# Earlier partial sums of the last 512 output rows, the turned exp sums first in TensorE's queue, and new scheduler settings, in a fused spectral-filter and attention kernel

## The chip, the cores and the metric

The kernel runs on one core of a Trainium2 chip. Its time is the device time of one launch in microseconds (us), and the figures quoted are medians of several launches. On one core most launches agree within 0.3%.

The engines are TensorE (PE in the profile; PEld is its weight loads), VectorE (DVE), ScalarE (ACT), GpSimd (POOL) and SyncE (SP). PSUM is the memory that matmuls write to; the program uses it as eight banks of 512 float32 columns. SBUF is the on-chip memory that holds everything else.

## The reference

Two independent problems on 2048 x 640 bf16 inputs are put side by side in one output of 2048 x 1280:

```python
def _A_ref(x, w_r, w_i):                       # spectral filter, columns 0:640
    X = rfft2(x.astype(float32)) * (w_r + 1j * w_i)
    return irfft2(X, s=(2048, 640)).astype(bfloat16)

def _B_ref(x, wqkv, wo):                       # attention, columns 640:1280
    H, Dh = 32, 20
    q, k, v = ...                              # from x @ wqkv
    p = softmax(q @ k.T * Dh ** -0.5)          # 32 heads of 2048 x 2048
    return (p @ v).transpose(...).reshape(2048, 640) @ wo
```

The softmax has 32 x 2048 x 2048 elements, and every one of them needs an exp. That sets the length of the kernel.

## The kernel before

The program is not written in its order of execution. A scheduler runs when the kernel is built: it keeps a simulated clock for each engine, asks at each step what that engine could do next, and fixes the order in each engine's queue. `occupy(engine, duration)` advances the simulated clock, so the durations in the code are assumptions. On the chip an engine works through its queue in this order and waits on semaphores: in the kernel before, a matmul whose input was ready at about 844.9 us ran only at 848.56, behind 28 others that stood ahead of it in TensorE's queue.

The attention is cut into 32 units: four blocks of 512 queries by eight groups (`g`) of four heads. Scores are made in tiles of 128 keys x 512 queries, 2048 of them. Most go through ScalarE's exp in groups of three and two tiles (PSUM banks 0 to 2, and 3 to 4). Some go in pairs through VectorE:

```python
def try_exp(self):
    i = self.nexp
    if i >= self.nqk or self.qk_t[i] > self.now or self.pt_free[i % NPT] > self.now:   # NPT = 6 buffers
        return False
    ...
    h = 3 * (i % 2)
    pt = self.PT[i % NPT][:, 0:512 * n]
    in_ = self.ps[:, h:h + n, :].rearrange("p b n -> p (b n)")
    self.P.add("act", lambda e: e.activation(pt, in_, AF.Exp, scale=SCALE, bias=-15.0 / LOG2E), ...)
```

The product with V goes to bank 6. At the end of a unit VectorE copies that bank out (`unit_copy`). For the units before the last one, the exp sums then take a way over DRAM, and the output product of each finished block of 512 queries runs as background work. The last unit (`u == 31`) has nothing to hide behind, so its end is a special path, the tail:

```python
def tail_jobs(self):                            # background, before the last exp
    for qb in range(2, 4):                      # row blocks 2 and 3 of the last 512 rows
        for half in range(2):                   # 320 output columns each
            for g in range(NG - 1):             # seven of the eight groups, summed in PSUM
                ... e.matmul(o, OTn[:, g, rows of qb], wo_pad[:, g, half], start=(g == 0), stop=(g == NG - 2))
            # one copy to SBUF:  self.part[:, qb - 2, half]
    # blocks 0 and 1 are summed in the tail itself, 2 x 2 x 7 = 28 matmuls:
    self.tail_op = [(0, half, g) for half in range(2) for g in range(NG - 1)] + [(1, half, g) ...]

def tail_pe(self):                              # TensorE's choice in the tail
    if self.tail_op:                            # 1. the 28 matmuls
        ...
        if ok:
            self.tail_mm(qb, half, g)
            return True
    ...                                         # 2. turned sums: osb (sums in one row of 32) by a
    #    selection matrix -> 128 x 16 in bank 2, so that VectorE takes 16 columns of reciprocals
    #                                             3. spread of 1/sum to all partitions ("tail_spread")
    #                                             4. last group's output matmuls, once VectorE has
    #                                                multiplied ("tail_norm", one per row block)

def tail_add(self, qb, half):                   # blocks 2 and 3: PSUM + kept part -> output rows
    self.P.add("dve", lambda e: e.tensor_tensor(o, a, b, ALU.add), ...)
    self.occupy("dve", 470.0)
```

"Turned" means that TensorE brings the exp sums, which lie along rows, onto all 128 partitions (the rows of the on-chip memories), so that VectorE can take the reciprocals of 16 columns and not of whole rows. "Spread" means that TensorE then brings each reciprocal to all the partitions that have to be multiplied by it.

At the very end VectorE computes a flag: whether any exp sum left the range in which this fast program is exact. All engines load the flag and branch on it, and a second, slower program follows for the case that it is set. With this input it never is.

```python
fast = FK(nc, arena, *args, cfg=dict(LEAD=28, T_A=760000.0, WARM_SHARE=0.45, RUN=1, PVQ=12, WIN=1000.0,
          T_X=40000.0, AHEAD=45e3, T_RB=9000.0, SKIP=1, ALONE=1200.0, PVB=10, PTB=6, WARMUP=10))
```

These settings steer the scheduler. `WARM_SHARE` and `WIN` say when filler matmuls with no use but to keep TensorE's clock up are put in, and hold some background work back too. `LEAD`, `SKIP`, `ALONE` and `T_X` govern which score tiles go to VectorE, and `T_A` how fast the spectral problem is worked off.

## Time and profile before

The median of the first three runs was 860.89 us (860.78 to 861.23). The profiled launch divides as follows. "Exps" means the exp instructions on ScalarE, L1783 of the kernel; they carry the whole kernel.

| part of the profiled launch | us |
|---|---|
| span | 859.8 |
| until the first exp starts | 10.56 |
| first exp start to last exp end | 831.15 |
| of that, gaps between exps (ScalarE idle) | 8.39 |
| last exp's end to the end of the program (tail) | 18.05 |

A group line of the profile has busy time and the mean duration in ns after the bar, then the idle time of that engine before these instructions and whom it waited for. A timeline line has start, duration, engine, source line, operation, shapes and count; in brackets stands the idle time before it and who ended it. When a line merges several instructions, its duration runs from the first start to the last end.

### The profile page before, as it was taken

Reading aid. Unit: us, or ns where it says so; the run is one execution under the profiler, and the core shown is the slowest. Engines: PE = TensorE matmul, PEld = TensorE weight load, DVE = VectorE, ACT = ScalarE, POOL = GpSimd, SP = SyncE. Lnnn points to the kernel's source line nnn. Section 1 sums busy time; section 2 is a strip of 40 time slices with the busy share of each in tenths; the row PEclk is TensorE's granted clock in tenths of the full one; section 3 lists DMA queues with packets and bytes.
Section 4 is the critical chain, followed back from the end, with each engine's and each line's share of the span. In section 5 each row is a group of like instructions: output and inputs, shape, how many; then the busy total and the mean of one; then the engine's idle time right before and its main releaser. Section 6 shows DMA issues by size and latency. Waiting matters only on the chain.

```text
span 859.8 us, 18764 instructions
## 1 busy us (share of the span) xinstructions
PE 809.8 (94%) x8000; PEld 281.2 (33%) x8000; DVE 765.2 (89%) x1485; ACT 830.1 (97%) x738; POOL 2.9 (0%) x8
## 2 busy tenths in 40 slices
PE   8999999999899999999999998989999999999995
PEld 4334323334233333322233422222333332333323
DVE  3487799999897999999998899999999889999972
ACT  6999999999999999999999999999999999999992
POOL 1000000000000000000000000000000000000000
PEclk9999999999999999999999999999999999999998
DMA  7420000001401000010101000001011101011210
GB/s 243 120 61 14 2 14 14 14 14 27 152 14 45 14 14 14 6 47 14 50 14 37 23 6 9 14 14 49 5 38 50 37 22 33 6 37 45 75 44 34
DMA packets 34462, 32.00 MB, mean 37 GB/s; under 512 B 13892, under 2 KB 28484, under 8 KB 34372
## 3 DMA queue, kind: packets, MB, share of 16 engines
q1 hardware_dynamic: 33796, 30.21, 11.3%
q8 instruction: 64, 1.05, 0.5%
q10 hardware_dynamic: 576, 0.52, 0.2%
q14 instruction: 26, 0.21, 0.1%
HBM read 24.97 MB, written 5.50 MB: 35 GB/s over the span
## 4 chain that ended last, share of the span: by engine, by line
ACT 58%; DVE 26%; PE 15%; issue 1%; DVEq 0%; POOL 0%; POOLq 0%
ACT arena L1783 57%; DVE arena L227 6%; DVE arena L1857 4%; PE ps L1766 4%; DVE arena L1253 3%; PE ps L2032 2%; PE ps L1952 2%; DVE arena L1897 2%; DVE arena L1901 2%; DVE arena L1904 2%; PE ps L1581 1%; DVE arena L1895 1%; DVE arena L1899 1%; DVE arena L1893 1%; PE ps L1662 1%
## 5 line engine op out<-in xcount | busy, mean ns | idle before, releaser
L1783 ACT ACTIVATE arena<-ps 128x1536 bf16<-128x1536 f32 x725 | 822.8, 1355 | 7.4 <-PE ps L1766 6.8
L1766 PE MATMUL ps<-arena 32*128 32x512 bf16 x2048 | 309.8, 385 | 26.8 <-ACT arena L1783 14.4
L1952 PE MATMUL ps<-arena 128*32 128x512 bf16 (+3 forms) x2048 | 190.5, 386 | 0.8 <-DVE arena L227 0.4
L1857 DVE TENSOR_SCALAR arena<-ps 128x512 uint16<-128x512 f32 x236 | 162.1, 688 | 13.3 <-PE ps L1766 12.2
L1766 PEld LDWEIGHTS ps<-arena 32*128 32x128 bf16 x2048 | 77.5, 91 | 264.9 <-ACT arena L1783 185.3
L227 DVE CAST arena<-ps 128x320 bf16<-128x320 f32 (+3 forms) x190 | 104.2, 548 | 19.8 <-PE ps L1610 9.9
L1646 PE MATMUL ps<-arena 128*32 128x512 bf16 x964 | 89.6, 389 | 1.6 <-DVE arena L1972 1.4
L1897 DVE TENSOR_TENSOR arena<-arena 128x1024 f16<-128x1024 uint16 x118 | 81.3, 690 | 1.0
L1901 DVE TENSOR_TENSOR arena<-arena 128x1024 f16<-128x1024 f16 x118 | 81.1, 688 | 0.9
L1904 DVE TENSOR_TENSOR arena<-arena 128x1024 uint16<-128x1024 uint16 x118 | 80.9, 687 | 0.2
L1952 PEld LDWEIGHTS ps<-arena 128*32 128x32 bf16 (+1 forms) x2048 | 46.1, 93 | 74.3 <-issue 61.3
L1525 DVE TENSOR_SCALAR arena<-ps,arena 128x512 bf16<-128x512 f32 x61 | 49.3, 808 | 19.9 <-PE ps L1581 14.1
L227 DVE COPY arena<-ps 128x1024 bf16<-128x1024 bf16 (+4 forms) x59 | 42.4, 721 | 19.3 <-PE ps L540 7.7
L1581 PE MATMUL ps<-arena 128*32 128x512 bf16 x640 | 51.0, 383 | 0.7 <-DVE arena L227 0.6
L1895 DVE TENSOR_SCALAR arena<-arena 128x1024 f16<-128x1024 uint16 x118 | 49.8, 424 | 0.7
L1899 DVE TENSOR_SCALAR arena<-arena 128x1024 f16<-128x1024 uint16 x118 | 49.7, 422 | 0.6
L1893 DVE TENSOR_SCALAR arena<-arena 128x1024 uint16<-128x1024 uint16 x118 | 49.8, 424 | 0.5
L1662 PE MATMUL ps<-arena 128*32 128x512 bf16 x640 | 49.3, 382 | 0.4 <-DVE arena L227 0.3
L1646 PEld LDWEIGHTS ps<-arena 128*32 128x32 bf16 x964 | 23.2, 94 | 47.2 <-issue 38.9
L1334 PE MATMUL ps<-arena 128*128 128x320 bf16 (+1 forms) x192 | 38.3, 303 | 0.1
L2032 PE MATMUL ps<-arena 128*128 128x320 bf16 x192 | 36.7, 302 | 0.2 <-DVE arena L1857 0.2
L1610 PE MATMUL ps<-arena 128*128 128x80 bf16 (+1 forms) x320 | 32.2, 236 | 0.0
(74 smaller groups left out, 438.6 us busy)
## 6 DMA issues: line engine op xcount, KB each, us to landing
arena<-rscr SPq DMA_DIRECT2D x31, 256.0 KB
arena<-in_A_x_dram SPq DMA_DIRECT2D x4, 640.0 KB, 6.9
out_dram<-arena SPq DMA_DIRECT2D x4, 640.0 KB, 3.4
out_dram<-arena SPq DMA_DIRECT2D x15, 160.0 KB, 1.8
arena<-f_ciCS SPq DMA_DIRECT2D x8, 256.0 KB, 2.9
arena<-arena SPq DMA_DIRECT2D x124, 2.0 KB, 1.7
arena<-in_B_x_dram SPq DMA_DIRECT2D x3, 640.0 KB, 5.5
arena<-f_cslab SPq DMA_DIRECT2D x2, 768.0 KB, 4.4
```

The lines of the kernel that those rows point to most:

```text
L227: return eng.tensor_copy(out, in_)
L1581: inst = e.matmul(ps[32 * j:32 * j + 32, bank, :], self.wqkv[:, cbv, c:c + 32], r_, start=st, stop=sp, tile_position=(0, 32 * j))
L1646: i = e.matmul(ps[32 * j:32 * j + 32, 6, :], z, k, start=False, stop=False, skip_group_check=True, tile_position=(0, 32 * j))
L1766: inst = e.matmul(ps[:, bank, :], kt_[32 * j:32 * j + 32, g, kt * 128:(kt + 1) * 128], q[32 * j:32 * j + 32, :], start=True, stop=True, ti ...
L1783: self.P.add("act", lambda e: e.activation(pt, in_, AF.Exp, scale=SCALE, bias=-15.0 / LOG2E), r=[("ps", h + k) for k in range(n)], w=[("PT ...
L1857: self.P.add("dve", lambda e: e.tensor_scalar(v, in_, 1024.0 * SCALE * LOG2E, 31743.0, ALU.mult, ALU.min), r=[("ps", bank)], **({"w": [key ...
L1893: t = self.x_op(n, one, lambda e: e.tensor_single_scalar(sh, v, 6, ALU.logical_shift_left), [kv], [ka], "x_s")
L1895: t = self.x_op(n, one, lambda e: e.tensor_scalar(b16, sh, -2.0 ** -24, 2.0 ** -8, ALU.mult, ALU.add), [ka], [kb], "x_l")
L1897: t = self.x_op(n, two, lambda e: e.tensor_tensor(b16, sh, b16, ALU.mult), [ka, kb], [kb], "x_q")
L1901: t = self.x_op(n, two, lambda e: e.tensor_tensor(b16, b16, a16, ALU.mult), [ka, kb], [kb], "x_h")
L1904: t = self.x_op(n, two, lambda e: e.tensor_tensor(v, v, b16, ALU.add), [kb, kv], [kv], "x_w")
L1952: inst = e.matmul(ps[32 * j:32 * j + m, 6, :], va[:, kt, 21 * h:21 * h + m], pt, start=st, stop=sp, tile_position=(0, 32 * j))
```

## The change

The intent is to shorten the tail. There are four parts.

1. Six groups (instead of seven) of **all four** row blocks are summed as background work and kept in SBUF. In blocks 0 and 1 the kept part goes back into PSUM by a float32 matmul with the identity; in blocks 2 and 3 VectorE adds it.
2. In `tail_pe` the turned sums and the spread now come ahead of the remaining output matmuls.
3. Three assumed durations of the scheduler's clock are altered.
4. Seven settings are altered.

The background sums are also asked for one unit earlier (`u == 29`), at another priority (-4.0e4 instead of -1.0e5; not in the cut below).

```diff
-                return (mkev, 0.0, 1.0417 * ne + 124, kw, ...)          # spectral multiply, assumed ns
+                return (mkev, 0.0, 1.0417 * ne + 155, kw, ...)
...
-        self.part = a.f32(zB, 2 * 640).rearrange("p (q n) -> p q n", q=2)
+        self.part = a.f32(zB, 4 * 640).rearrange("p (q n) -> p q n", q=4)
...
-        t = self.occupy("dve", 270.0)                                   # unit_recip
+        t = self.occupy("dve", 110.0)
...
-        if u == 30:
+        if u == 29:
             self.tail_jobs()
...
-        for qb in range(2, 4):
+        for qb in range(4):
...
-                for g in range(NG - 1):
+                for g in range(NG - 2):
...
-        self.tail_op = [(0, half, g) for half in range(2) for g in range(NG - 1)] + [(1, half, g) ...]
+        self.tail_op = [(qb, half, g) for qb in range(2) for half in range(2) for g in (-1, NG - 2)]
...
+        if g == -1:
+            l, r_, rk = self.idf, self.part[:, qb, half * 320:(half + 1) * 320], [("idf",), ("part", qb, half)]
...
     def tail_pe(self):
-        if self.tail_op:            # the 28 matmuls: first
-            ...
         ... turned sums, spread, last group's matmuls (now with group six for blocks 2 and 3) ...
+        if self.tail_op:            # what is left of the output product: last
+            ...
...
-        self.occupy("dve", 470.0)                                       # tail_add
+        self.occupy("dve", 400.0)
...
-  LEAD=28, T_A=760000.0, WARM_SHARE=0.45, WIN=1000.0, T_X=40000.0, SKIP=1, ALONE=1200.0
+  LEAD=32, T_A=600000.0, WARM_SHARE=0.43, WIN=1400.0, T_X=30000.0, SKIP=0, ALONE=500.0
```

## The prediction

> **What bounds the kernel now.** I read the page first, then the instruction groups with their shapes kept apart, then ScalarE's timeline over the whole span, and last the timeline of all engines in the final 20 us. On the page, two lines name the bound: the chain that ended last, and the costliest group.
>
> ```profile
> ACT 58%; DVE 26%; PE 15%; issue 1%; DVEq 0%; POOL 0%; POOLq 0%
> L1783 ACT ACTIVATE arena<-ps 128x1536 bf16<-128x1536 f32 x725 | 822.8, 1355 | 7.4 <-PE ps L1766 6.8
> ```
>
> L1783 is the exp of the attention scores, read out of PSUM. It is busy 822.8 of 859.8 us and ScalarE stands idle before it for only 7.4 us. (TensorE's 94% is no rival bound: VectorE and TensorE have gaps in which nothing is lost, and ScalarE's wait on TensorE is 6.8 us in all.) By shape, the exps are of two sizes, three score tiles of 512 columns or two:
>
> ```profile
> L1783 ACT ACTIVATE arena<-ps 128x1536 bf16<-128x1536 f32 x362 | 566.2, 1564 | 7.3 <-PE ps L1766 6.8
> L1783 ACT ACTIVATE arena<-ps 128x1024 bf16<-128x1024 f32 x363 | 415.5, 1146 | 0.1
> ```
>
> 362 x 3 + 363 x 2 = 1812 tiles go through ScalarE; the rest of the 2048 (236) are done in pairs on VectorE (118 pairs). The busy times overlap, so 566.2 + 415.5 is more than 822.8; I need starts apart, and take them from ScalarE's timeline:
>
> ```profile
> 10.56 6.89 ACT L1783 ACTIVATE arena<-ps 128x1536 bf16<-128x1536 f32 x6 [0.49 <-PE ps L1766]
> ...
> 276.18 239.93 ACT L1783 ACTIVATE arena<-ps 128x1536 bf16<-128x1536 f32 x212 [0.83 <-PE ps L1766]
> ...
> 691.37 150.34 ACT L1783 ACTIVATE arena<-ps 128x1536 bf16<-128x1536 f32 x133 [0.42 <-PE ps L1766]
> ```
>
> 212 exps without a gap, 106 of each size, take 239.93 us, so a pair of a large and a small one costs 2.264 us. With the two means 0.418 us apart that is about 1.34 us and 0.92 us. The first exp starts at 10.56, the last ends at 691.37 + 150.34 = 841.71; so the kernel is 10.6 us of front, 831.1 us of exps with some 8 us of gaps in them, and **a tail of 18.1 us** (841.71 to 859.8) in which ScalarE hardly works. The tail is where the change acts:
>
> ```profile
> 842.27 0.69 DVE L1972 COPY arena<-ps 128x512 f32<-128x512 f32 x1 [1.88 <-PE ps L1952]
> ...
> 843.11 0.96 PE L2112 MATMUL ps<-arena 128*128 128x4 f32 x8
> ...
> 844.32 0.25 DVE L2146 RECIPROCAL arena<-arena 128x16 f32<-128x16 f32 x1
> 844.60 0.50 DVE L2151 COPY arena<-arena 128x256 f32<-128x256 f32 x2
> ...
> 844.74 3.98 PE L2084 MATMUL ps<-arena 128*128 128x320 bf16 x28 [0.52 <-ACT arena L226]
> ...
> 848.56 0.61 PE L2123 MATMUL ps<-arena 128*128 128x128 f32 x4
> 849.20 0.29 DVE L2163 TENSOR_TENSOR arena<-arena,ps 128x128 bf16<-128x128 f32 x1 [4.01 <-PE ps L2123]
> ```
>
> The reader is to see: the last unit's result is copied (L1972), its exp sums are turned by TensorE (L2112), VectorE takes reciprocals, and their spread to all partitions (L2123) could start by about 844.9. But 28 matmuls of the output product (two row blocks x two halves x seven groups) stand ahead of it in TensorE's queue, started only at 844.74, and the spread runs at 848.56. VectorE's multiply waits 4.01 us for it. So about 3.6 us of the tail is queue order.
>
> **What the Trainium skill says.** "TensorE: Matmul & The Clock Gate", Back-to-back issue gap, has N/2.4 + 2.5 ns for a warm matmul: 136 ns for 320 columns. The trace has 3.98 us for 28 with one drain, 0.136 us from start to start: it agrees. "FP8 and Floating Point Precision", TensorE Precision Notes, says that true FP32 takes four passes; the trace shows each fp32 matmul as two rows, 0.107 to 0.112 us apart at 128 columns, twice what 128 bf16 columns would take by the formula above: four cycles a column in all, the same cost. The same TensorE page, under the HAM clock gate, has half clock after an idle window of about 3.4 us. This matters because the change alters how many filler matmuls are issued, and this trace does show one such drop:
>
> ```profile
> 230.00:232.00 2.00, 2.00 (x18) 0.41 (x16) 0.00 (x0) 1.77 (x2) 0.00 (x0) 0.53 0.04 6
> ```
>
> (the 0.53 is the granted clock; ScalarE's gap there is 0.45 us, so one drop is cheap). "ScalarE: Activation LUTs", What ACT_TABLE_LOAD costs, has 0.833 ns per column for an ACTIVATE: 0.427 us for 512 columns against the 0.418 us difference above; it agrees within 2%.
>
> **The change, part by part.** The order of the changed program was compared with that of the one before, which gives counts, not times.
>
> 1. *Partial sums.* The last 512 output rows are 4 row blocks x 2 halves. Before, blocks 2 and 3 had seven groups summed early and kept in SBUF, and blocks 0 and 1 were summed (2 x 2 x 7 = 28 matmuls) in the tail. Now six groups of all four blocks are summed as background work (8 jobs of 6 matmuls and one copy each) before the last exp; in blocks 0 and 1 the kept part returns by an fp32 identity matmul, in blocks 2 and 3 VectorE adds it, as before. Background cost: 48 matmuls instead of 28, and six more VectorE copies of 0.40 us (2.4 us), beside running exps: hidden.
> 2. *Identity matmuls.* By four cycles a column, 320 columns cost about 0.54 us (an estimate from the 128-column rows). Four of them. The first stands before the last product with V, hidden by the last exp. The second and third with one bf16 matmul of 0.136 us stand after that product and before the turned sums: 0.54 + 0.14 + 0.54 = 1.22 us. The last with its bf16 neighbours (0.81 us) stands after the sums, under VectorE's reciprocal and copy.
> 3. *New tail, from the last exp's end, t0.* Last product with V starts at t0 + 0.09, as now; TensorE is free at t0 + 0.42; 1.22 us of identity work ends at t0 + 1.64. The copy of L1972 is done at t0 + 1.25, so the sums start at 1.64 (now 843.11, t0 + 1.40: 0.24 later). From the first sum to the first reciprocal's input 1.0 us, to the first spread copy 0.5, its 0.29 and the hand-over with an fp32 weight load 0.1: spread at t0 + 3.55, with TensorE free since 1.64 + 0.80 + 0.81 = 3.25. From spread to multiply 0.64, as now: t0 + 4.2. Now it is 849.20 - 841.71 = 7.49. **Gain 3.3 us**, less about 0.1 because blocks 2 and 3 now bring group six in the tail too (one 0.136 us matmul ahead of the first add). The three spread-and-multiply turns, the adds at 0.40 us apart, the stores, the flag and the end (10.6 us after the first multiply) stay. The tail is then about 14.9 us instead of 18.1: **-3.2 us**.
> 4. *Settings of the build-time scheduler.* They reorder nearly every row, but the totals move little: VectorE takes 116 pairs of score tiles instead of 118, so ScalarE has 1816 tiles: 363 large, 363 small and one of 512 columns. That adds one large exp (1.34) and one single (0.92 - 0.42 = 0.49): **+1.8 us** on the bound. Filler matmuls fall from 301 to 238, about 14 us of TensorE time, hidden. VectorE loses two pairs, each about 2.8 us by start-to-start times of 0.33 and 0.60: hidden too, as VectorE isn't the bound.
> 5. *Gaps between exps.* Now about 8 us: bursts of other matmuls between two score groups (near 74, 82, 275 and 690 us), the clock drop at 232, and small ones between 516 and 629 us where VectorE's spectral multiplies hold TensorE's queue. Counting the matmuls between neighbouring score groups in both orders, at measured spacings, I find after the start-up three bursts above 1.5 us before (1.79, 1.53, 1.52) and three after (1.64, 1.95, 1.74): no visible difference. I take no change from counting and give 0.5 us to the likelihood that settings like these are kept for shortening such gaps.
>
> Sum: 860.89 - 3.2 + 1.8 - 0.5 = 859.0 us.
>
> **The rivals.** (a) *The fillers were needed*: with 63 fewer, TensorE's clock drops more often and score groups come late. For: one drop is seen now. Against: it cost about half a microsecond, and TensorE waits for ScalarE's buffers 185 us in all, so it has slack. Four more drops would make 861. (b) *The new tail is bound by something else*: the identity matmuls wait for the last VectorE copies or for a PSUM bank, or spread comes no earlier as VectorE is late. Against: VectorE idled 4.9 us just before its last copies; for: six more copies stand in that stretch. Then the gain is 1 to 2 us and the time about 861. (c) *The background sums disturb the last exps*: TensorE's queue is in order, and each new job waits for VectorE to free one of two banks; 700 to 842 us has no gap now, so it can only get worse: up to +2 us. (d) *The settings remove most gaps*: half of 8 us gone gives 855.5.
>
> **Range and chances.** The two terms that I can work out, -3.2 and +1.8, are each good to some 0.3 us; the gaps are good to about 2 us either way. So 859.0, with 856.2 to 861.4 for 8 in 10. Two per cent is 17 us, twice all gaps together; neither side of it is in sight without a fault: 0.01 faster, 0.98 same, 0.01 slower.
>
> **What would show it.** The timeline after: from the last exp's end to the span's end about 14.9 us; a single 512-column exp last; the spread's matmuls about 3.5 us after that end, with no long run of bf16 matmuls ahead; fp32 identity rows of about 0.27 us each, two to an instruction. The groups: 363, 363 and 1 exps, busy about 824.6. ScalarE's idle before exps near 7 us. I am wrong if the exps' gaps go below 4 or above 10 us, if the identity matmuls cost twice my estimate, or if the granted clock falls in many slices.

## The result and the profile after

The changed kernel took **858.07 us** (median of four runs, 857.72 to 858.53); the kernel before took 860.84 us in the same rounds. The ratio is 0.9968, with a 95% interval from 0.9951 to 0.9985. Ratios here and below are made from the runs of both kernels in the same batch; they are not quite the ratios of the medians. The result is correct. The difference of about 2.8 us is small but resolved.

The profiled launches, side by side:

| part | before | after | difference |
|---|---|---|---|
| until the first exp | 10.56 | 10.50 | -0.06 |
| first exp start to last exp end | 831.15 | 830.85 | -0.30 |
| tail | 18.05 | 14.95 | -3.10 |
| span | 859.8 | 856.3 | -3.5 |
| exps | 725 | 727 | +2 |
| exps' busy time | 822.8 | 823.8 | +1.0 |
| gaps between exps | 8.39 | 7.04 | -1.35 |
| filler matmuls | 301 | 238 | -63 |

The spans of two single launches differ by 3.5 us, the timed runs by 2.8 us. That is no contradiction: the profiled launch of the kernel before took 861.56 us, 0.7 us more than its median. I read the single launches for the parts only.

The first lines are from the page of the kernel after: the chain that ended last by engine, and the costliest group.

```profile
ACT 56%; DVE 30%; PE 11%; issue 1%; POOL 0%; DVEq 0%; POOLq 0%
L1783 ACT ACTIVATE arena<-ps 128x1536 bf16<-128x1536 f32 x727 | 823.8, 1349 | 6.0 <-PE ps L1766 4.8
```

The bound is the same as before: 823.8 of 856.3 us are exps. Next the same group with its shapes kept apart.

```profile
L1783 ACT ACTIVATE arena<-ps 128x1536 bf16<-128x1536 f32 x363 | 566.1, 1559 | 5.9 <-PE ps L1766 4.8 <-PE ps L1952 0.4
L1783 ACT ACTIVATE arena<-ps 128x1024 bf16<-128x1024 f32 x363 | 413.5, 1139 | 0.1
```

That is 363 large and 363 small exps, with one single-tile exp on top: 363 x 5 + 1 = 1816 tiles against 1812. ScalarE's timeline after shows where the gaps were:

```profile
81.95 430.25 ACT L1783 ACTIVATE arena<-ps 128x1536 bf16<-128x1536 f32 x380 [1.24 <-PE ps L1766]
...
689.19 152.16 ACT L1783 ACTIVATE arena<-ps 128x1536 bf16<-128x1536 f32 x135 [0.56 <-PE ps L1766]
```

From 81.95 us on, 380 exps run without a gap, for 430.25 us, so a pair of a large and a small one takes 2.264 us, exactly as before. In the kernel before the same stretch had gaps at 232.22 (0.45 us, the clock drop) and at 276.18 (0.83 us). The gaps of 100 to 300 us sum to 1.28 us before and to 0.15 us after; from 510 to 655 us they are 3.14 and 2.98 us, practically unchanged. The stretch that dropped before is shown by the windows view of after (PE, PEld, DVE, ACT and POOL busy, each with its count; then granted clock, DMA share, GB/s):

```profile
230.00:232.00 2.00, 1.77 (x18) 0.39 (x10) 2.00 (x5) 2.00 (x3) 0.00 (x0) 1.00 0.38 36
```

The granted clock is 1.00 there, where it was 0.53. Over the whole launch the mean granted clock is 0.999 after and 0.995 before, with 63 fillers fewer; but nearly half of this difference is the idle end, where the clock is at 0.50 for the last 5.0 us before and the last 1.9 us after. The drop at 230 us is not in every launch of the old order either: in the profile of `reorder_only` below, whose order is that of the kernel before up to the tail, the clock is 1.00 from 226 to 236 us and the gaps are 7.96 us.

Now the tail, from the timeline of all engines in the kernel after. The last exp ends at 841.35.

```profile
840.64 0.94 PE L2087 MATMUL ps<-arena 128*128 128x320 f32 x3
...
841.85 1.48 PE L2087 MATMUL ps<-arena 128*128 128x320 f32 x5
841.96 0.69 DVE L1972 COPY arena<-ps 128x512 f32<-128x512 f32 x1 [4.99 <-PE ps L1952]
...
843.16 0.95 PE L2099 MATMUL ps<-arena 128*128 128x4 f32 x8
...
844.65 0.49 DVE L2156 COPY arena<-arena 128x256 f32<-128x256 f32 x2
844.99 0.52 PEld L2110 LDWEIGHTS ps<-arena 128*128 128x128 f32 x4 [0.52 <-DVE arena L2156]
844.99 0.71 PE L2110 MATMUL ps<-arena 128*128 128x128 f32 x4
845.74 0.29 DVE L2168 TENSOR_TENSOR arena<-arena,ps 128x128 bf16<-128x128 f32 x1 [0.60 <-PE ps L2110]
```

The run of 28 matmuls ahead of the spread is gone. The spread (L2110) starts at 844.99, 0.34 us after the reciprocals' copy started: it waits for VectorE, not for a queue. The multiply (L2168) waits 0.60 us for it instead of 4.01. What is left ahead of the turned sums (L2099) is the group of five L2087 rows: two identity matmuls of two rows each, and one bf16 matmul between them.

One more thing has moved. In the kernel before, the last eight of the early matmuls and two copies of their sums on ScalarE ran after the last exp, and the 28 matmuls waited for the second copy (until 844.69). In the kernel after, all 48 early matmuls and their copies are done by 833.7.

### The profile page after: what moved, and what is told of

Read it like the earlier page. It is cut to its first block, busy times and chain, and to the rows that moved or that the text cites. A ratio compares the mean times of both kernels' runs of the same rounds, so it can differ in the third digit from the quotient of the medians.

```text
span 856.3 us, 18371 instructions
## 1 busy us (share of the span) xinstructions
PE 796.4 (93%) x7802; PEld 277.2 (32%) x7828; DVE 760.6 (89%) x1475; ACT 830.3 (97%) x738; POOL 2.9 (0%) x8
## 4 chain that ended last, share of the span: by engine, by line
ACT 56%; DVE 30%; PE 11%; issue 1%; POOL 0%; DVEq 0%; POOLq 0%
ACT arena L1783 56%; DVE arena L227 5%; DVE arena L1857 5%; PE ps L1766 3%; DVE arena L1253 3%; DVE arena L1897 2%; DVE arena L1901 2%; DVE arena L1525 2%; DVE arena L1904 2%; PE ps L1952 2%; PE ps L1581 2%; DVE arena L2318 1%; DVE arena L1893 1%; DVE arena L1895 1%; DVE arena L1899 1%
## 5 line engine op out<-in xcount | busy, mean ns | idle before, releaser
L1783 ACT ACTIVATE arena<-ps 128x1536 bf16<-128x1536 f32 x727 | 823.8, 1349 | 6.0 <-PE ps L1766 4.8
L1766 PE MATMUL ps<-arena 32*128 32x512 bf16 x2048 | 312.1, 384 | 35.6 <-ACT arena L1783 21.8
L1952 PE MATMUL ps<-arena 128*32 128x512 bf16 (+3 forms) x2048 | 192.9, 385 | 0.7 <-DVE arena L227 0.4
L1857 DVE TENSOR_SCALAR arena<-ps 128x512 uint16<-128x512 f32 x232 | 157.4, 684 | 10.2 <-PE ps L1766 9.8
L1766 PEld LDWEIGHTS ps<-arena 32*128 32x128 bf16 x2048 | 77.7, 91 | 268.5 <-ACT arena L1783 184.1
L1897 DVE TENSOR_TENSOR arena<-arena 128x1024 f16<-128x1024 uint16 x116 | 79.5, 685 | 0.9
L1904 DVE TENSOR_TENSOR arena<-arena 128x1024 uint16<-128x1024 uint16 x116 | 79.3, 683 | 0.4
L1646 PE MATMUL ps<-arena 128*32 128x512 bf16 x808 | 75.4, 386 | 1.1 <-DVE arena L1972 1.1
L1952 PEld LDWEIGHTS ps<-arena 128*32 128x32 bf16 (+1 forms) x2048 | 47.4, 93 | 76.8 <-issue 63.3
L227 DVE COPY arena<-ps 128x1024 bf16<-128x1024 bf16 (+4 forms) x65 | 45.1, 697 | 14.1 <-PE ps L540 7.7
L1581 PE MATMUL ps<-arena 128*32 128x512 bf16 x640 | 53.1, 384 | 1.0 <-DVE arena L227 0.6
L1895 DVE TENSOR_SCALAR arena<-arena 128x1024 f16<-128x1024 uint16 x116 | 48.8, 421 | 1.0
L1662 PE MATMUL ps<-arena 128*32 128x512 bf16 x640 | 49.0, 382 | 0.6 <-DVE arena L227 0.4
L1899 DVE TENSOR_SCALAR arena<-arena 128x1024 f16<-128x1024 uint16 x116 | 48.9, 421 | 0.4
L1646 PEld LDWEIGHTS ps<-arena 128*32 128x32 bf16 x808 | 19.4, 93 | 39.1 <-issue 34.0
```

The source lines that it names most:

```text
L227: return eng.tensor_copy(out, in_)
L1581: inst = e.matmul(ps[32 * j:32 * j + 32, bank, :], self.wqkv[:, cbv, c:c + 32], r_, start=st, stop=sp, tile_position=(0, 32 * j))
L1646: i = e.matmul(ps[32 * j:32 * j + 32, 6, :], z, k, start=False, stop=False, skip_group_check=True, tile_position=(0, 32 * j))
L1766: inst = e.matmul(ps[:, bank, :], kt_[32 * j:32 * j + 32, g, kt * 128:(kt + 1) * 128], q[32 * j:32 * j + 32, :], start=True, stop=True, ti ...
L1857: self.P.add("dve", lambda e: e.tensor_scalar(v, in_, 1024.0 * SCALE * LOG2E, 31743.0, ALU.mult, ALU.min), r=[("ps", bank)], **({"w": [key ...
L1897: t = self.x_op(n, two, lambda e: e.tensor_tensor(b16, sh, b16, ALU.mult), [ka, kb], [kb], "x_q")
```

## The experiments

Eighteen microseconds of tail and 831 of exps can trade against each other, so the first question is which part of the change carries the 2.8 us. My theory was the prediction's: the tail gives about 3 us, and four more tiles on ScalarE and a few gaps nearly cancel. The rivals were that the settings give the gain by fewer gaps, that order alone gives it (the identity matmuls being mere decoration), and that fillers had been holding the clock. Kernels that are compared in one batch ran on the same chip; the kernel before had medians of 860.77, 860.98, 860.94 and 861.0 us in the four batches.

### tail_only: the new tail with the old settings and assumed durations

```diff
--- after
-                return (mkev, 0.0, 1.0417 * ne + 155, kw, ...)
+                return (mkev, 0.0, 1.0417 * ne + 124, kw, ...)
-        t = self.occupy("dve", 110.0)
+        t = self.occupy("dve", 270.0)
-  LEAD=32, T_A=600000.0, WARM_SHARE=0.43, WIN=1400.0, T_X=30000.0, SKIP=0, ALONE=500.0
+  LEAD=28, T_A=760000.0, WARM_SHARE=0.45, WIN=1000.0, T_X=40000.0, SKIP=1, ALONE=1200.0
```

> The new tail alone, with the scheduler's settings and assumed VectorE costs of before: the program is that of before up to the last 20 us (118 VectorE pairs, 725 exps). My theory, that the tail is worth 3.1 us on its own and the settings only shift gaps between exps: exps from 10.5 to about 841.7 as before, tail 14.9 us, 857.7 us, so no slower than the full change. Rival 1, that the background sums disturb the last exps: a gap of 0.5 to 2 us appears after 785 us, 858.3 to 859.7. Rival 2, that the settings carry part of the gain: 858.5 or more with no such gap.

It took 858.08 us, ratio 0.9968 (0.9954 to 0.9982): the same as the whole change. The profile has 725 exps and 118 pairs, as before, gaps of 8.89 us and a tail of 15.56 us. The tail is 0.6 us longer than in the whole change, and here the last matmuls and a store of the spectral problem run beyond the last exp, as they do not in the whole change. Sixteen output matmuls instead of twelve stand behind the last spread, and VectorE's adds begin 7.27 us after the last exp instead of 6.94. What of this causes the 0.6 us I have not isolated. The clock drop near 232 us is back, with a larger gap than before:

```profile
232.54 43.05 ACT L1783 ACTIVATE arena<-ps 128x1536 bf16<-128x1536 f32 x38 [0.92 <-PE ps L1766]
```

This is one line of ScalarE's timeline; the 0.92 us is the gap at the drop, 0.45 in the kernel before. So the tail alone accounts for the measured gain.

### settings_only: the old tail with the new settings and assumed durations

```diff
--- after
     (tail_jobs, tail_mm, tail_pe, tail_add, part and "u == 30" as in the kernel before;
      the new cfg, "+ 155" and "occupy("dve", 110.0)" kept)
```

> The settings and assumed VectorE costs of the change, with the tail of before (117 pairs, 726 exps). My theory: exp busy time 0.5 to 1 us longer than before, gaps between exps about 1 to 2 us less, tail still 18.1 us with 28 matmuls ahead of the spread: 860.0 to 861. Rival, that the settings are a gain of themselves: 859.0 or less.

It took 860.27 us, ratio 0.9995 (0.9982 to 1.0009): nothing that the runs can resolve. The profile shows what stands behind the zero: 726 exps, gaps of 6.96 us, first exp start to last exp end 829.81 us, tail 17.87 us. The settings take some 1.4 us of gaps away and load one more exp on ScalarE.

### reorder_only and reorder_bank6: order alone, without the early partial sums

`reorder_only` keeps the old partial sums (28 matmuls in the tail) and the old settings, and takes only the new order of `tail_pe`.

```diff
--- after
-        if u == 29:
+        if u == 30:
-        for qb in range(4):            ...  for g in range(NG - 2):
+        for qb in range(2, 4):         ...  for g in range(NG - 1):
-        self.tail_op = [(qb, half, g) for qb in range(2) for half in range(2) for g in (-1, NG - 2)]
+        self.tail_op = [(0, half, g) for half in range(2) for g in range(NG - 1)] + [(1, half, g) ...]
     (settings and assumed durations as in the kernel before; tail_pe's new order kept)
```

> The kernel before with one edit: in the tail, the 28 output matmuls of row blocks 0 and 1 are asked for after the spread of the reciprocals and the last group's matmuls, not before. Nothing is removed. If queue order alone is worth the 3.3 us (what the prediction's first reading of the 4.01 us wait suggests): 857.6. If the removed work matters too, since these matmuls then end the kernel together with their ScalarE copies and stores: the spread starts about 3.5 us after the last exp as in the change, but only about 1 us is won: 859.8, and the last matmuls of the product come after the spread.

The result was **wrong** (relative error 0.165), so its time (860.75 us, ratio 0.9997) is no evidence. My edit was at fault: in the new order the sums of half block (0, 1) are still in bank 7 when half block (3, 1) starts there, and the start flag throws them away. Both are writers of the same bank. `reorder_bank6` mends it:

```diff
--- reorder_only
-    TAIL_BANK = {..., (3, 0): 4, (3, 1): 7}
+    TAIL_BANK = {..., (3, 0): 4, (3, 1): 6}
```

> As reorder_only, whose result was wrong because two sums then shared a PSUM bank; the last half block now has bank 6 of its own, so the result should be correct. The wrong run gave 860.75 us, no gain. Theory, that removed work and not queue order is what counts: spread about 3.4 us after the last exp as in the change, but the 28 matmuls then run after it with the last ScalarE copies behind them: 859.5 to 861. Rival, that the wrong run was slow for its fault: 857.6 to 858.5.

It took 859.32 us and was correct, ratio 0.9984 (0.9972 to 0.9996): about half of the gain. The timeline of its tail (the last exp ends at 841.41) shows why it is only half:

```profile
844.73 0.64 PE L2107 MATMUL ps<-arena 128*128 128x128 f32 x4
845.41 0.29 DVE L2161 TENSOR_TENSOR arena<-arena,ps 128x128 bf16<-128x128 f32 x1 [0.60 <-PE ps L2107]
...
846.95 4.79 PE L2084 MATMUL ps<-arena 128*128 128x320 bf16 x34
...
851.64 0.75 ACT L2188 CAST arena<-ps 128x320 bf16<-128x320 f32 x2 [0.94 <-PE ps L2084]
```

The spread starts 3.32 us after the last exp, even a little earlier than in the whole change (3.64). But the matmuls that stood ahead of it now stand behind it, 34 in a row for 4.79 us, and the last output rows are copied only at 851.64. The tail is 16.06 us. What ends this kernel is the flag: its small matmul stands behind the 34 in TensorE's queue and runs at 851.67, though its inputs were ready at 849.96. In the branch records of the packed trace TensorE's branch follows from 853.13 to 857.11, while the last store was waited for by 854.4.

So order moves the work, and the early partial sums remove it from the tail. Two things are not shown. No run has the early sums in the old order; in the kernel after, the last output matmul ahead of the spread starts at 844.64 us and the spread (844.99) waits for VectorE, so the sums without the new order might do as well. And no run has the new order with the flag's matmul ahead of the 34, so "half of the gain" holds for this place of the flag only.

### sums_first and sums_first_warm: no identity matmul ahead of the turned sums

In the kernel after, the sums stand behind 1.3 us of identity work (841.85 to 843.16). `sums_first` holds it back until the sums are in the queue, and starts the first ones a little earlier.

```diff
--- after, in tail_pe
+            if self.u_pv == 32 and self.tail_b is None:
+                return False
-                ok = (self.u_act == 32 and ...
+                ok = ((self.u_act == 32 or (self.u_act == 31 and len(self.rem[31]) < self.cfg["LEAD"])) and ...
```

> The changed kernel with the identity matmuls kept away from the place between the last product with V and the turned sums (both halves of block 0 before that product, block 1 after the sums). If the 1.2 us of identity work there delays the sums: they start 1.3 us after the last exp rather than 1.8, 857.5 against 858.07. If it's hidden because something else follows (the spread waits for the block 1 work now put after the sums): 858.0.

It took 858.87 us, ratio 0.9977 (0.9964 to 0.9991): no better than the change, and its tail was 17.28 us, 2.3 us **longer**. The sums do start early, 1.25 us after the last exp's end at 841.25 instead of 1.81. This line of its timeline also shows the idle time that made room for them:

```profile
842.50 1.05 PE L2099 MATMUL ps<-arena 128*128 128x4 f32 x8 [0.80 <-DVE arena L1972]
```

The windows view of the same kernel has the price, in the granted clock (the third number from the right):

```profile
842.00:843.00 1.00, 0.50 (x5) 0.50 (x5) 0.45 (x1) 0.00 (x0) 0.00 (x0) 1.00 0.00 0
...
844.00:845.00 1.00, 1.00 (x4) 0.66 (x3) 0.55 (x3) 0.00 (x0) 0.00 (x0) 0.69 0.00 0
845.00:846.00 1.00, 1.00 (x5) 0.76 (x3) 0.00 (x0) 0.00 (x0) 0.00 (x0) 0.50 0.00 0
```

Two microseconds in which TensorE was busy half the time (0.52 of 841 to 842, 0.50 of 842 to 843) stand ahead of it: the granted clock falls to 0.50 at about 844.4 us (0.69 is the mean of that microsecond) and stays there until about 851 us, through all the rest of the output product. No single idle stretch was longer than 0.80 us.

This profile is of the slowest of five launches (860.33 us, mean clock 0.994). One more took 860.15 us at 0.994; the other three took 857.83 to 858.87 us at 0.996 and 0.997. So the drop probably came in two launches of five, and the 2.3 us are the price in a launch that has it, not in the median.

`sums_first_warm` is the test of that reading. It puts four filler matmuls into the hole and changes nothing else:

```diff
--- sums_first, in tail_pe
+                if self.tail_fill:                   # starts at 4
+                    self.tail_fill -= 1
+                    self.dummy(3)
+                    return True
                 return False
```

> As sums_first (858.87 us, with runs from 857.83 to 860.33), with four filler matmuls of 512 columns in the 0.8 us in which TensorE stood idle before the turned sums. Theory, that sums_first lost because TensorE's clock fell to 0.50 of full speed in the tail after those idle stretches: granted clock 1.00 through the tail, tail near 14.4 us, 857.6 us and a spread between runs of less than 1 us. Rival, that keeping the identity work out of the way is no gain for another reason: 858.1 or more with the clock at 1.00.

In the profiled launch the clock stayed at 1.00 until the work was done and the tail came back to 14.99 us; the time was 858.27 us, ratio 0.9964 (0.9952 to 0.9976). None of its six launches has a mean clock under 0.997. So the drop came with the hole, as far as one profile each and six launches can show it. The run also shows that earlier sums alone gain nothing over the change (14.99 against 14.95 us of tail): what is saved ahead of the sums is owed behind them. Its timeline shows it, the last exp having ended at 842.36:

```profile
843.63 1.04 PE L2101 MATMUL ps<-arena 128*128 128x4 f32 x8
844.52 1.46 PE L2087 MATMUL ps<-arena 128*128 128x320 f32 x5
...
845.82 0.61 PE L2112 MATMUL ps<-arena 128*128 128x128 f32 x4
```

The identity rows now stand between the sums and the spread, and the spread starts 3.46 us after the last exp, against 3.64.

### both and both_first: the next waits of the tail

The tail of the kernel after has two more waits of the same kind. The spreads of blocks 1 to 3 share bank 4 with the multiplies that read it, so they go in three turns. And the flag is computed after the last add, so that the branch comes last: in the trace's branch records TensorE's branch takes 4.02 us (851.93 to 855.95, with the program's end at 856.3), other engines' 0.05 to 0.07 us. The last store was waited for by 852.4, so the branch ends this kernel; in the kernel before it does so too (855.27 to 859.40, end at 859.76). `both` uses two banks for the spreads and computes the flag as soon as the last exp sums are known:

```diff
--- after
-                l, idf, o = self.rb[:, c], self.idf, ps[:, 4, c]
+                l, idf, o = self.rb[:, c], self.idf, ps[:, 4 + qb // 2 * 2, c]        # banks 4 and 6
...
-        self.dve_urgent.append((self.now + 2000.0, ... "sums" ...))
+        self.dve_urgent.append((self.now + 800.0, cert))      # "sums", then flag_a(): the five small operations
...
+                if qb == 1:
+                    self.flag_b()                              # flag's matmul, after block 1's output matmuls
...
+        if qb == 3:
+            self.dve_urgent.insert(0, (self.tf["dve"], self.flag_c))     # flag, before the adds
```

> The changed kernel with two more edits of the tail: the spread of row blocks 2 and 3 in another PSUM bank, so that it doesn't wait for the first two multiplies, and the overflow flag computed before the last adds instead of after them. In the trace of the change the turns of spread and multiply take 2.2 us from the first multiply to the last's end, of which about 1.2 us are hand-overs, and from the last add to the flag 1.1 us, after which TensorE's branch takes 4.0 us. If both are on the path that ends the kernel: 855.5 to 856.5. If the stores' landing sets the end instead: 857 or more. If the clock falls in the tail as in sums_first: runs up to 2 us apart.

It took **855.84 us**, ratio 0.9938 (0.9926 to 0.995), correct. From first to last exp the profile is that of the change to 0.02 us (830.87), with the same gaps of 7.04 us; the tail is 11.91 us. The timeline of its tail (last exp's end at 841.32):

```profile
844.97 1.16 PE L2110 MATMUL ps<-arena 128*128 128x128 f32 x8
...
845.72 0.93 DVE L2176 TENSOR_TENSOR arena<-arena,ps 128x128 bf16<-128x128 f32 x4
...
847.12 0.14 DVE L2484 TENSOR_SCALAR arena<-arena 1x1 int32<-1x1 f32 x1
847.19 1.86 SPq L2196 DMA_DIRECT2D out_dram<-arena  x3
847.32 1.69 DVE L2185 TENSOR_TENSOR arena<-ps,arena 128x320 bf16<-128x320 f32 x4
```

All four spreads run in one go and the four multiplies follow in 0.93 us. The flag (L2484) is there at 847.12, ahead of the adds and not behind them, and TensorE's branch (3.52 us, from 848.17) runs beside the last adds and stores: it ends at 851.69, and the wait for the last store at 852.2. Which of the two edits is worth how much I did not separate.

`both_first` is `both` together with `sums_first_warm`, and the last identity matmul of block 1 held until the four spreads are out:

```diff
--- both
+            if (qb, half) == (1, 1) and self.n_spread < 4:
+                return False
+            if self.u_pv == 32 and self.tail_b is None:
+                ...                                            # four fillers, as in sums_first_warm
```

> The kernel of the run both (855.84 us, tail 11.9 us) with no identity work between the last product with V and the turned sums: block 0's before that product, four fillers in the idle stretch, only half a block's identity work between the sums and the spread, the rest after the spread. In both, the sums start 1.8 us and the spread 3.65 us after the last exp. Theory, that this chain still sets the end: sums at 1.3, spread at 3.2 us, tail 11.5 us, 855.4 us. Rival, that with the flag out of the way the row blocks' stores end the kernel and block 1 is now stored last: spread earlier as said, but 855.8 or more.

It took 855.25 us, ratio 0.9937 (0.9923 to 0.995), with a tail of 11.81 us. Against `both` that is equal within the intervals. The spread starts 3.19 us after the last exp, 0.46 earlier than in `both`, and the gain is lost again at the end: ScalarE's last copy of block 1 starts only at 848.94 us, after VectorE's last add (848.52), and the last store waits for it. Both versions beat the kernel before by about 0.6% and the change by about 0.3%; of the two, `both` is the smaller edit.

### nofill, warm_old, both_lead and old_costs: what the settings hold up

The prediction gave the gaps 2 us either way. To see what the settings are worth, I moved them by themselves. `nofill` has fewer fillers:

```diff
--- after
-  WARM_SHARE=0.43
+  WARM_SHARE=0.30
```

> The changed kernel with the share below which filler matmuls are issued set to 0.30 instead of 0.43: 115 fillers instead of 238, the same 116 pairs and 727 exps. Rival (a) of the prediction, that fillers are needed: several drops of the granted clock, each with a gap of 0.5 to 1 us between exps: 860 or more. If the change's fillers are more than needed: 858.1, no drop. My theory: between, 1 to 4 drops, 859 us.

It took 875.36 us, ratio 1.0177 (1.0151 to 1.0203). There are 115 fillers instead of 238, the gaps are 18.07 us and the mean granted clock is 0.974. The page's clock line, in tenths of full speed for 40 slices of the span:

```profile
PEclk9999999999889999999999999999969999999998
```

The slices 11 and 12 (218 to 261 us), 30 (632 to 653 us) and the last one are below full speed; in the kernel after every slice has a 9. The gaps from 225 to 253 us fall in the first of these stretches. Yet not all of the 17 us over the change can be put down to the clock: the same setting also decides when background work is let in, and the gaps from 510 to 655 us (10.75 us) are as large in a kernel below (`both_lead`, 11.04 us) whose clock was 1.00 there. Over its six launches the mean clock and the time go together, from 0.980 with 872.58 us to 0.959 with 880.58 us.

`warm_old` is the change with only the two filler settings put back:

```diff
--- after
-  WARM_SHARE=0.43, WIN=1400.0
+  WARM_SHARE=0.45, WIN=1000.0
```

> The changed kernel with only the two filler settings of before (share 0.45 over 1000 ns): 305 fillers instead of 238, with the same 116 pairs and 727 exps. If fewer fillers shortened the gaps between exps: gaps of 8 us or more instead of 7.0, 859 us or more. If filler counts above what the clock needs are free: gaps as bursts in the order have them (2.01, 2.24, 1.98, 2.86 us against 1.64, 1.95, 1.74), 859 to 860, and no drop of the clock in either; the cause is then the order and not the fillers.

It took 866.17 us, ratio 1.0061 (1.0047 to 1.0075), with more fillers (305), a mean clock of 0.996, and gaps of 15.60 us, one of them of 5.12 us at 545.3. More fillers are thus no cure, and the two old values, which did no harm among the other old ones, do harm here.

`both_lead` is `both` with one setting put back:

```diff
--- both
-  LEAD=32
+  LEAD=28
```

> The kernel of the run both, with one setting back at its value of before (a VectorE pair may be started while 28 score tiles of a unit are left, not 32): 120 pairs instead of 116, so 362 large and 361 small exps, eight tiles fewer on ScalarE. If exps on ScalarE are what the middle of the kernel is made of, they take 3.6 us less (1.34 + 2 x 0.92 + 0.49, less rounding). Its order has one burst of 3.5 us of other matmuls between two score groups (near 550 us) that the other order has not, worth a gap of about 2.5 us. Theory: 854.7. If pairs cost more than they give because VectorE then delays TensorE: 856 or more.

It took 862.75 us, ratio 1.0027 (1.0013 to 1.004), although VectorE takes 120 pairs instead of 116, so that ScalarE has eight tiles fewer. Its tail is 12.06 us, as in `both`; the gaps are 16.86 us, and 6.54 us of them are one gap. This is its timeline around it:

```profile
544.12 1.42 DVE L1253 TENSOR_TENSOR arena<-ps,arena 128x512 bf16<-128x512 f32 x2
...
545.46 0.87 DVE L1258 TENSOR_TENSOR arena<-arena 128x512 bf16<-128x512 bf16 x2
546.25 0.68 DVE L1972 COPY arena<-ps 128x512 f32<-128x512 f32 x1
...
546.39 0.61 PE L1265 MATMUL ps<-arena 128*128 128x512 bf16 x2 [1.54 <-DVE arena L1258]
...
546.99 0.83 PE L1952 MATMUL ps<-arena 128*32 128x512 bf16 x12
547.03 0.69 DVE L227 CAST arena<-ps 128x512 bf16<-128x512 f32 x1
547.44 2.37 ACT L1783 ACTIVATE arena<-ps 128x1536 bf16<-128x1536 f32 x2 [6.54 <-PE ps L1952]
```

The last products with V of a unit (L1952, at 544.45) had waited for VectorE's half of a pair (L1904, from 543.34). The unit's result (bank 6) is then copied by VectorE only at 546.25, behind the spectral multiplies L1253 and the adds or subtracts L1258. The next unit's products with V (L1952) write that bank, so they wait for the copy, while TensorE also stands 1.54 us at L1265 for L1258. Until those products have read the exps' output buffers, ScalarE has no buffer to write: the exp is released by L1952, not by its scores (L1766). This chain is read from the releasers in the trace; no run tried it alone. In `both` the same background work comes in a slightly different order in this stretch, and there is no gap over 0.14 us from 512.59 to 569.8 us. The clock is 1.00 in both kernels there.

`old_costs` puts back the two assumed durations and nothing else:

```diff
--- after
-  1.0417 * ne + 155   /  occupy("dve", 110.0)
+  1.0417 * ne + 124   /  occupy("dve", 270.0)
```

> The changed kernel with the two assumed VectorE costs of before (the spectral multiplies 31 ns shorter, reciprocal and sums 270 instead of 110 ns): 115 pairs, 364 large and 363 small exps, 1818 tiles on ScalarE. If the assumed costs were what shortened the gaps: gaps between 512 and 650 us of 4 us or more instead of 3.0. My theory, that they did nothing there: those gaps 2.5 to 3.5 us, exps 0.85 us longer (0.92 + ... one large for one small and one single), time 858.5 to 860, by where the bursts of this order fall (2.86 and 1.77 us at two places).

It took 864.58 us, ratio 1.004 (1.0026 to 1.0053): gaps of 12.35 us, with 2.97 us at 517.7 and 1.94 us at 697.7, and 115 pairs, and a tail of 16.48 us in which the clock was at 0.50 from 852.9 us to the end. This profile is of the slowest of five launches (866.63 us at 0.993; the others 863.87 to 864.66 us at 0.997 and 0.998). The assumed durations steer only the order, and yet they are worth 6.5 us in the medians. I can't say that they are "better": `tail_only`, with the old durations and the old settings, is as fast as the whole change. What these four runs show together is that the schedule is one of a set of unequal neighbours. My own expectations for them (859, 859 to 860, 854.7 and 858.5 to 860 us) were all too low, by 5 to 16 us.

## Why the prediction was right

- **The tail.** The predicted 14.9 us was measured as 14.95, and it was so by the steps given. From the last exp's end (t0 = 841.35): turned sums at 1.81 (predicted 1.64), spread at 3.64 (3.55), first multiply at 4.39 (4.2). An identity matmul took 0.54 to 0.64 us where the estimate was 0.54: its first pass took 0.37 us instead of 0.27 in the two places where it follows the product with V, and not after a bf16 matmul of the output product. That is 0.10 of the 0.17 us by which the sums are late; the rest is that the group starts at 0.50 and not at 0.42. The four cycles a column did not follow from the lines that the prediction read: its rows of 4 columns are 0.112 us apart like those of 128, so something other than columns may have set that distance. The rows of 320 columns, 0.269 us apart in the kernel after, bear it out. The multiply came 0.19 us later than reckoned, and the 0.1 us set aside for group six does not show: from the first multiply to the end it is 10.56 us in both kernels. That these two nearly cancel is luck, of 0.1 us. `tail_only` and `settings_only` show that all of the resolvable gain is the tail's.
- **The exps.** Four more tiles were predicted to add 1.8 us, and the count of 363, 363 and 1 came as foretold. At the unchanged 2.264 us a pair that is the sum. The busy time rose by 1.0 us only (predicted 824.6, measured 823.8). An exp that follows another without a gap overlaps its end, and most of the difference lies there: exps that started late but still within that overlap lost 6.1 us instead of 6.9, counted against the median distances of 1.331 and 0.904 us. That there are fewer fresh starts after a gap (20 instead of 22) does not explain it, as what they cost beyond their gaps is 3.5 us in both.
- **The gaps.** This term was mis-sized. The prediction took 0.5 us off as a "likelihood"; the gaps shrank by 1.35 us, and with the late starts above the stretch of exps took 830.85 us where 831.15 + 1.8 - 0.5 = 832.45 was expected: 1.6 us less. The gaps shrank from 100 to 300 us (1.28 to 0.15 us), where the kernel after had neither the clock drop nor the late group at 275 us, and not in the spectral stretch, whose multiplies the new assumed duration describes (3.14 to 2.98 us). Up to 1.1 of the 1.6 us is the launch: `reorder_only`, in the old order but without the drop at 230 us, took 830.04 us for the same stretch. In the timed runs all of this is inside the noise.
- **"About 3.6 us of the tail is queue order."** As an allocation this was wrong, though the sum was right. `reorder_bank6` moves the spread forward by 3.5 us (from 6.86 to 3.32 us after the last exp) and gains only about 1.4 us of time (a ratio of 0.9984), or 2.0 us of tail. Without the early partial sums the 28 matmuls come back behind the spread, and there they hold up the flag.
- **Rival (a), the fillers.** It didn't hold for this change: with 63 fillers fewer the profiled launch shows no drop while exps run. But the prediction's reasons against it were weak. The 185 us are the waits of the weight loads; TensorE's matmuls themselves (L1766) waited for ScalarE 14.4 us. And the drop that it took for the effect of an idle window followed none: TensorE was busy for 1.44 and 1.36 us of the two stretches of 2 us before it (226 to 230 us). The rival isn't empty, as `nofill` shows; the edge lies somewhere between 238 and 115 fillers, or in the order that comes with them.
- **Rivals (b) and (c).** No wait for VectorE's copies or a bank stands ahead of the identity matmuls, and 700 us to the last exp has no gap, as before. Both were rightly put aside.
- **Rival (d)** was right in its direction (8.39 to 7.04 us) and not in its size.
- **The width of the gaps.** "Good to about 2 us either way" was far too narrow for a schedule whose order changes throughout. The neighbours `warm_old`, `both_lead` and `old_costs` have gaps of 12 to 17 us, and took 6 to 8 us longer than their parents. That the measured gaps stayed inside was luck as far as the prediction's working goes: counting bursts could not have told this set of settings from its neighbours. It supposed that such settings are kept for their short gaps.

## What to carry to other kernels

When one engine carries a kernel, look at what is left after its last instruction: there every wait counts in full, and an order that puts the shortest way to the last engine first was worth only half here while the work that it displaced still stood ahead of the flag. Keep the matmul engine busy in holes of such a tail, as a half-busy stretch of 2 us cost 2.3 us in the launch that was profiled, and compute whatever the program branches on before the end. Where a build-time schedule is changed as a whole, judge a single setting only on the chip: three neighbours here differed by 6 to 8 us for reasons that no count of instructions showed.

## What the Trainium skill lacked or had wrong

- "TensorE: Matmul & The Clock Gate", A second HAM failure mode, says that frequent short idle times of TensorE between groups of matmuls make the clock fall, but gives no size, and the page's other sections go by an idle window of about 3.4 us. Here two microseconds at half load (TensorE busy 0.52 and 0.50 us of one microsecond each, the longest idle time 0.80 us) were followed by a granted clock of 0.50 from about 844.4 to 851 us, and the tail was 17.28 us instead of 14.95. With four filler matmuls in the hole the profiled launch kept 1.00 (tail 14.99 us). In the traces fourteen such drops come in mid-work; TensorE was busy for 0.63 to 0.72 of the 3.41 us before each, so none followed an idle window. Other stretches of that length had no drop after them at 0.62 to 0.67 (in `nofill`), so no threshold follows.
- "Runtime: NRT & Kernel Launch", Instruction fetch mechanics, says that a taken branch out of the fetched window stalls, without a figure for the stall or the engines concerned. In the branch records of these traces the branch at the end takes TensorE 4.13 us before and 4.02 us after, and the other engines 0.05 to 0.07 us. That instruction fetch is the cause is not shown by any run here; with an early flag the branch ran beside the last stores.
- No page says how far an order of in-order queues can carry a late buffer. Here a copy that frees one PSUM bank stood behind 2.1 us of other VectorE work (544.12 to 546.25), itself after a late pair, and ScalarE stood still for 6.54 us with no drop of the clock.
